# Score matmuls on strips of 32 columns, pads among the last scatters, and the bank of a third tile

## The chip, the cores and the metric

One core of a Trainium2 chip runs one program. The metric is the device time of one execution in microseconds (us), lower is better. TensorE (PE) multiplies, with its weight loads shown apart as PEld; VectorE is DVE, ScalarE is ACT, GpSimd is POOL, and SyncE (SP) issues most of the DMAs. POOL issues the indirect DMAs (scatters) and the pads, on a DMA queue of its own (q0); SP's loads run on q1.

## The reference

The input is `x` of 8 x 2880 tokens with 192 values each. Two steps follow each other:

- a convolution: each of 8 heads weights the last 7 tokens with a softmax over 7 given numbers: `out[s] = sum_k w[s,h,k] * x[s-6+k]`;
- a mixture of experts on the 23040 tokens that come out. `g_logits = x @ w_group` picks one of 4 groups by argmax, `e_logits = x @ w_expert[g]` one of 4 experts in it, so 16 experts in all. The token's result is `relu(x @ w1[g,e]) @ w2[g,e]` (192 to 1024 to 192), times the two softmax weights of the choices.

The choice needs 4 + 16 = 20 scores per token, each a product over 192 values.

## The kernel before, in words

The tokens are taken in 15 groups of 1536 (12 rows of 128 partitions). For each group a front computes the convolution (mostly on DVE), then `logits` (line 387): the rows are turned by TensorE so that the 192 values lie on partitions, values 0 to 127 as one turned tile per row and the remaining 64 of two rows together as a third. `score` multiplies the turned tiles (`xTs`) with the score weights `wr`. `wr[:, 0, :]` are the weights of values 0 to 127, `wr[:, 1, :]` and `wr[:, 2, :]` hold those of the remaining 64 in their upper or lower half and zeros in the other, 32 columns each. In the product the 32 score columns of four rows lie on the four strips of 32 partitions of one bank. `ranks` (line 446) turns scores into a place for each token: a DRAM buffer `rows` holds the tokens sorted by expert, and twelve scatters of POOL (`scatter_row`, line 518, issue line 523) put a group's tokens there. A scatter reads its places from a small copy `ix` (line 522), of which there are three in turn.

`table` (line 537) makes from the counts the list of blocks whose rows are complete at the end of a round (14 rounds; ROUNDS lists at which group each ends and how many blocks of which width it runs). In the last round the remaining rows run, so each expert's run of rows is padded with 256 rows of zeros first: 16 DMAs of POOL (the loop at lines 592 to 598, issue line 595), each with a place read by POOL from a tile `pfi` (line 593).

The blocks run meanwhile, in `blocks` (line 1072). A block loads its rows (`xb`, line 825) and the expert's weights by SP, turns the rows (`prep_x`, line 919; the tile `tpx` or `tp`, transposes at lines 935 and 936), and has two products per unit: `gemm1` (line 961) and `gemm2` (1007, or 1009 and 1010). From round 12 on a block is not `whole`: w2 is loaded into `raw` or `xin` (line 855), cut into a high part by ACT (line 884) and a low part by DVE (line 892). Likewise the turned rows: ACT writes the high part `xh` (line 941), DVE subtracts it and writes the low part `xl` (line 892); both read the bank in which the turned columns lie. A block of three tiles turns two of them at the second unit of the block before it, and the third tile later. Blocks of three tiles are one in round 10 and, in the last round, three full ones and seven with a short third tile; so the last round has nine transitions from a block of three tiles to another.

The order of instructions on PE, ACT, DVE and SP is written out by a planner in the kernel (`clk` holds its clock of each engine, `run` adds a cost, `arrive` says when a round's rows may be loaded); each of these engines runs its list in order. POOL's order is set by the framework from what is ready. Dependencies between the pads and loads of earlier rounds are declared away (`written_once`), so that only the last round's row loads wait for the pads.

Two pieces of code that the change touches:

```python
tp = ps_t.tile([P, 2, 1, P], F32, name="tp") if beside else ps_x.tile([P, 2, 2, P], F32, name="tpx")[:, :, 0:m]
...
if nxt.nt > 2 and u == (last // 2 + 1 if cur.wide else 1):
    prep_x(nxt, 2, not cur.wide)
```

`ps_t` and `ps_x` have one bank each.

Of the kernel before, what the change touches and what calls it, by code (L numbers as in the profile page):

```python
# [12 lines left out]
I32 = mybir.dt.int32  # L13
# [29 lines left out]
def conv_moe_kernel(ctx: ExitStack, tc: tile.TileContext, x, wgen, w_group, w_expert, w1, w2, out):  # L43
# [221 lines left out]
    def run(eng, cost, *deps):  # L265
        clk[eng] = max([clk[eng]] + [d + HOP for d in deps]) + cost
        return clk[eng]
# [10 lines left out]
    def round_of(g):  # L278
        return next(r for r in range(NR) if g < ENDS[r])
# [107 lines left out]
    def logits(g, o):  # L387
        n = WIDTHS[g]
        xrow = o.xrow
        early = g < FIRST  # L390
        pause = lambda t: UNIT if state["begun"] and t > clk["pe"] + 0.9 else NEXT
        yield Chunk(o, 1)
        new_lt = lambda: ps_y.tile([P, SG // 4, P], F32, name="py0") if g == FIRST - 1 else ps_l.tile([P, SG // 4, P], F32, name="pl")
        lt = new_lt() if early else None

        xTs = rt.tile([P, SG // 4, 2, 3, P], F32, name="xT")

        def score(q0, q1):
            for w in range(2):
                nc.tensor.matmul(  # L400
                    lt[2 * w * LW:2 * (w + 1) * LW, q0:q1, :], lhsT=wr[:, 1:3, :].rearrange("p a l -> p (a l)"), rhs=xTs[:, q0:q1, w, 2, :],
                    start=True, stop=False, tile_position=(0, 2 * w * LW))
            for j in range(4):
                nc.tensor.matmul(  # L404
                    lt[j * LW:(j + 1) * LW, q0:q1, :], lhsT=wr[:, 0, :], rhs=xTs[:, q0:q1, j // 2, j % 2, :],
                    start=False, stop=True, tile_position=(0, j * LW))

        txTs, scored = [], 0
        for s2 in range(0, n, 2):
            if o.chunks <= s2 // SC:  # L410
                yield Chunk(o, s2 // SC + 1)
            if s2 % SC == 0:
                rem = rt.tile([P, SC, HP], F32, name="rem")
                nc.scalar.copy(out=rem, in_=xrow[s2 // SC][:, :, P:D])
                txTs += [run("act", 0.4, clk["dve"])] * 2
                yield pause(txTs[-1])
            ttp = run("pe", 0.35, txTs[-2])
            tp = ps_t.tile([P, 3, P], F32, name="tp") if s2 % 4 == 0 else ph_tile(0, [P, 3, P]) if early else ps_l.tile([P, SG // 4, P], F32, name="pl")
            row = xrow[s2 // SC][:, s2 % SC:s2 % SC + 2, :]
            for u in range(2):  # L420
                nc.tensor.transpose(out=tp[:, u, :], in_=row[:, u, 0:P], identity=ident)
            nc.tensor.transpose(out=tp[:, 2, :], in_=rem[:, s2 % SC:s2 % SC + 2, :].rearrange("p s d -> p (s d)"), identity=ident)
            if early and s2 % 4 == 0 and s2:
                run("pe", 0.5, txTs[-1])
                score(s2 // 4 - 1, s2 // 4)
                scored = s2 // 4
            nc.scalar.copy(out=xTs[:, s2 // 4, s2 % 4 // 2], in_=tp)
            txTs.append(run("act", 0.48, ttp))
            yield NEXT if s2 < n - 2 else pause(txTs[-1])
        lt = lt or new_lt()  # L430
        run("pe", 0.1 + 0.4 * (n // 4 - scored), txTs[-1])
        score(scored, n // 4)
        lts = xTs[:, 0].rearrange("p w u t -> p (w u) t")[:, 0:3, :]
        nc.scalar.copy(out=lts, in_=lt)
        tlt = run("act", 0.48, clk["pe"])
        yield pause(tlt)
        lp = ps_l.tile([P, SG // 4, P], F32, name="pl")
        for u in range(n // 4):
            nc.tensor.transpose(out=lp[:, u, :], in_=lts[:, u, :], identity=ident)
        run("pe", 0.35, tlt)  # L440
        ls = rt.tile([P, SG, NL], F32, name="ls")[:, 0:n, :]
        nc.scalar.copy(out=ls, in_=lp.rearrange("p q (j l) -> p (q j) l", l=LW)[:, 0:n, 0:NL])
        run("act", 0.4, clk["pe"])
        ranking.append([ranks(g, o, ls, Until(clk["act"] + LATE[0 if early else 1])), None])

    def ranks(g, o, ls, tls):
# [61 lines left out]
        pi = rt.tile([P, SG], I32, name="posi", bufs=2)[:, 0:n]  # L508
        nc.vector.scalar_tensor_tensor(out=pi, in0=ps, scalar=-1.0, in1=ps, op0=ALU.mult, op1=ALU.max)
        yield TINY  # L510
        for s in range(n):
            run("pool", 2.2 if g in SPACED else 1.28, clk["dve"])
            scatter_row(pi[:, s:s + 1], xrow[s // SC][:, s % SC, :], round_of(g), g in SPACED)
        if g + 1 in ENDS:
            yield from table(round_of(g))
        o.routed = True

    def scatter_row(idx, src, r, spaced):
        ix = idx
        if spaced:  # L520
            ix = new_ix()
            nc.gpsimd.tensor_copy(out=ix, in_=idx)  # L522
        written_once(nc.gpsimd.indirect_dma_start(  # L523
            out=rows[:, :], out_offset=bass.IndirectOffsetOnAxis(ap=ix, axis=0),
            in_=src, in_offset=None, bounds_check=NROW - 1, oob_is_err=False), r)
# [11 lines left out]
    def table(r):  # L537
# [3 lines left out]
        def t(name, shape=(P, NE), dt=F32):  # L541
            return tb.tile(list(shape), dt, name=name)

        if last:
            pfi = t("pfi", (P, NE), I32)
            v.tensor_tensor(out=pfi, in0=cnt.rearrange("p e o -> p (e o)"), in1=lower, op=ALU.add)
        units, n2, tk = t("units"), t("n2"), t("tk")
        v.tensor_tensor(out=units, in0=cnt.rearrange("p e o -> p (e o)"), in1=per_unit, op=ALU.mult)
        v.tensor_tensor(out=units, in0=units, in1=origin[last], op=ALU.add)
# [38 lines left out]
            yield 0.6  # L588

        if last:  # L590
            pad2 = padding()
            for e in range(NE):
                rv = nc.gpsimd.value_load(pfi[0:1, e:e + 1], min_val=0, max_val=NROW - BK)
                run("pool", 1.04, clk["dve"])
                ins = nc.gpsimd.dma_start(out=rows[bass.ds(rv, BK), :].rearrange("(p t) c -> p t c", t=2), in_=pad2)
                written_once(ins, r)
                if e % 4 == 3:
                    yield NEXT
            for nb in (1, 2, 3, *CUT):
                arrive[r, nb] = clk["pool"] + 7.0  # L600

# [470 lines left out]
    def blocks(n0, n1, paced):  # L1072
# [99 lines left out]
        for i in range(len(units) + LAG):  # L1172
            if i < len(units):
                n, u = units[i]
                last = units_of(n) - 1
                gemm1(cur, u)
                queue.append((cur, u))
                nxt_at = i + last + 1 - u
                if nxt_at < len(units):
                    if u == 0:  # L1180
                        pump(units[nxt_at][0])
                        nxt = block(nxt_at)
                        prep_d(nxt)
                    if u == 1:
                        prep_x(nxt, 0)
                    if nxt.nt > 2 and u == (last // 2 + 1 if cur.wide else 1):
                        prep_x(nxt, 2, not cur.wide)
                if u == last and i + 1 < len(units):
                    cur = nxt
            asks = []  # L1190
            if i >= LAG:
                b, u = queue.pop(0)
                gemm2(b, u)
                if u == units_of(units[i - LAG][0]) - 1:
                    finish(b)
                    if b.cut:
                        gemm2_half(b)
                    if i - LAG + 1 < len(units):
                        asks.append(units[i - LAG][0] + 3)
            if i < len(units):  # L1200
                n, at = units[i]
                end = at == last
                if end and n + 4 < n1 and plain(n + 3) and not plain(n + 4):
                    ask_w(n + 4)
                    ask_w(n + 3)
                elif end and n + 3 < n1 and plain(n + 3):
                    ask_w(n + 3)
                elif end and n + 4 < n1 and plain(n + 2):
                    ask_w(n + 4)
                did = 0  # L1210
                for job in list(jobs):
                    m, part, h = job
                    if m > n + 2 or (part == 3 and (m > n + 1 or at < LAG)):
                        continue
                    must = end and m == n + 1
                    if not must and (did >= 1 or (m, part) in want or not ready(m)):
                        continue
                    jobs.remove(job)
                    work_split(job)
                    did += 1  # L1220
                state["unit"] += 1
                state["gemm"] += 1
            flush()
            if paced:
                fill(clk["pe"] + AHEAD[0 if cur.plain else 1 if cur.o.whole else 2])
            for a in asks:
                ask_x(a)
            pump()
# [45 lines left out]
```

## Time and profile before

| | |
|---|---|
| time, three runs | 1169.13, 1172.85, 1174.21 us; median 1172.85 |
| the profiled execution | 1175.43 us; its span from first to last instruction 1173.5 us |
| mean granted TensorE clock | 0.992 of full speed |
| PE busy | 1110.5 us, 95% of the span, 7865 matmul instructions |
| PEld busy | 1032.0 us, 88% |
| DVE busy | 950.4 us, 81% |
| ACT busy | 648.3 us, 55% |
| POOL busy | 580.0 us, 49% |
| DMA | 275.06 MB, mean 234 GB/s |

Busy shares are means over the whole span. An fp32 matmul of the source shows as two instructions, and the end of each is modelled, so the time from the start of one to the start of the next says more than a duration. The row of an instruction ends with the idle time of its engine before it and what released it; a releaser can be named wrongly ("issue" is time for which the profile shows none).

### The profile page before, as it was taken

What the parts mean: (1) busy time and instruction counts of PE and PEld (TensorE: products, weight loads), DVE (VectorE), ACT (ScalarE), POOL (GpSimd) and SP (SyncE); (2) the same over time, 40 slices, a digit from 0 to 9 for tenths busy, and PEclk for the clock granted to TensorE, in tenths of its full rate; (3) what the DMA queues carried; (4) which work ended last, traced back from release to release, by engine and by line L of the source; (5) the groups of instructions that cost most, each with busy time, mean ns of one, the idle gap of its engine ahead of it and who ended that gap; (6) DMA issues with size and microseconds to landing.
All of it is one profiled execution on the core that took longest, in us unless ns stands there. A gap on an engine that the chain in (4) does not pass through costs nothing.

```text
span 1173.5 us, 23791 instructions
## 1 busy us (share of the span) xinstructions
PE 1110.5 (95%) x7865; PEld 1032.0 (88%) x7865; DVE 950.4 (81%) x1682; ACT 648.3 (55%) x1307; POOL 580.0 (49%) x613
## 2 busy tenths in 40 slices
PE   5887998999999999999999999999999899999997
PEld 2444888899999999999999999999899899999997
DVE  8899997989888999989898989998673576655661
ACT  1341445555656555555565566556556676666672
POOL 7064184738256563758483837384746312222211
PEclk9998999999999999999999999999999999999999
DMA  5797999787778786888897868866768885665562
GB/s 175 224 308 221 295 311 297 237 286 226 274 223 265 232 293 216 272 244 262 250 297 221 282 213 270 270 206 195 238 191 231 250 241 159 186 183 192 162 211 68
DMA packets 84343, 275.06 MB, mean 234 GB/s; under 512 B 15297, under 2 KB 34161, under 8 KB 82417
## 3 DMA queue, kind: packets, MB, share of 16 engines
q1 hardware_dynamic: 64056, 229.77, 63.3%
q0 software_dynamic: 20032, 43.39, 12.2%
q8 instruction: 64, 1.05, 0.4%
q14 instruction: 71, 0.57, 0.1%
q10 hardware_dynamic: 120, 0.28, 0.1%
HBM read 225.83 MB, written 47.88 MB: 233 GB/s over the span
## 4 chain that ended last, share of the span: by engine, by line
PE 55%; issue 20%; DVE 10%; DMA 6%; POOL 5%; ACT 2%; another core or an unknown queue 1%; POOLq 1%; SPq 0%; DVEq 0%; ACTq 0%
PE py L1007 25%; PE ph L961 22%; POOL out L1045 5%; DVE pr L317 4%; DMA xin<-in_x 2%; DVE xrow L335 1%; DMA raw<-in_moe_w 1%; PE tpx L936 1%; DMA xb<-rows 1%; PE tpx L935 1%; PE ph L358 1%; PE pl L404 1%; PE pl L400 1%; DMA rows<-rem 1%
## 5 line engine op out<-in xcount | busy, mean ns | idle before, releaser
L961 PE MATMUL ph<-xh,wa 128*128 128x256 f32 (+3 forms) x1992 | 453.4, 303 | 0.0
L1045 POOL DMA_INDIRECT out<-y,xb x189 | 213.2, 1128 | 404.1 <-DVE y L1040 168.4
L1007 PE MATMUL py<-wc,hh 128*128 128x192 f32 x2160 | 399.6, 326 | 3.6 <-ACT y L1034 3.6
L961 PE MATMUL ph<-xl,wa 128*128 128x256 f32 (+3 forms) x1328 | 349.7, 284 | 0.6 <-DVE xl L892 0.6
L1007 PEld LDWEIGHTS py<-wc,hh 128*128 128x128 f32 x2160 | 344.8, 189 | 4.8 <-ACT y L1034 4.6
L961 PEld LDWEIGHTS ph<-xh,wa 128*128 128x128 f32 x1992 | 335.6, 189 | 9.9 <-issue 8.4
L970 ACT ACTIVATE hh<-ph 128x512 f32<-128x512 f32 (+2 forms) x296 | 165.6, 560 | 263.3 <-PE ph L961 218.8
L317 DVE TENSOR_TENSOR pr<-xin,wt 128x1152 f32<-128x1152 f32 x186 | 249.0, 1350 | 4.2 <-PE py L358 3.5
L961 PEld LDWEIGHTS ph<-xl,wa 128*128 128x128 f32 x1328 | 251.0, 189 | 1.0 <-DVE xl L892 0.9
L523 POOL DMA_INDIRECT rows<-xrow,ix x156 | 222.5, 1427 | 47.4 <-POOL ix L522 32.3
L335 DVE TENSOR_TENSOR xrow<-xrow,pr 128x1152 f32<-128x1152 f32 x144 | 194.6, 1351 | 0.7
L892 DVE SCALAR_TENSOR_TENSOR pr<-ph,hh 128x256 fp32r<-128x256 f32 (+2 forms) x128 | 65.7, 514 | 87.0 <-ACT hh L975 37.2
L892 DVE TENSOR_TENSOR wa<-raw,wa 128x1024 fp32r<-128x1024 f32 x83 | 101.3, 1220 | 23.7 <-ACT wa L868 19.4
L522 POOL COPY ix<-posi 128x1 int32<-128x1 int32 x156 | 73.3, 482 | 76.8 <-DMA rows<-xrow,ix 44.5
L1009 PE MATMUL py<-wc,hh 128*128 128x384 f32 x320 | 102.0, 363 | 0.0
L975 ACT ACTIVATE hh<-ph 128x256 fp32r<-128x256 f32 (+2 forms) x128 | 58.9, 460 | 56.9 <-PE ph L961 56.0
L868 ACT CAST wa<-raw 128x1024 fp32r<-128x1024 f32 x83 | 87.2, 1050 | 0.0
L877 ACT CAST wa<-raw 128x1024 fp32r<-128x1024 f32 x83 | 86.7, 1044 | 0.0
L1010 PE MATMUL py<-wc,pr 128*128 128x192 f32 x320 | 80.5, 252 | 0.0
L1034 ACT ACTIVATE y<-py,xb 128x192 f32<-128x192 f32 x175 | 66.3, 426 | 20.0 <-PE py L1007 15.4
L892 DVE TENSOR_TENSOR xl<-tpx,xh 128x512 fp32r<-128x512 f32 (+1 forms) x92 | 59.1, 643 | 13.3 <-ACT xh L941 11.9
L1010 PEld LDWEIGHTS py<-wc,pr 128*128 128x128 f32 x320 | 61.5, 192 | 0.0
(209 smaller groups left out, 1326.3 us busy)
## 6 DMA issues: line engine op xcount, KB each, us to landing
wc<-in_moe_w SPq DMA_DIRECT2D x73, 768.0 KB
raw<-in_moe_w SPq DMA_DIRECT2D x83, 512.0 KB
xin<-in_x SPq DMA_DIRECT2D x14, 1728.0 KB
raw<-in_moe_w SPq DMA_DIRECT2D x91, 256.0 KB
raw<-w1lo SPq DMA_DIRECT2D x83, 256.0 KB
xb<-rows SPq DMA_DIRECT2D x75, 194.0 KB
wa<-in_moe_w SPq DMA_DIRECT2D x24, 384.0 KB
raw<-in_moe_w SPq DMA_DIRECT2D x11, 768.0 KB
```

Source lines behind the costliest of these rows:

```text
L317: nc.vector.tensor_tensor(out=dst, in0=o.xin[:, c0 + k:c0 + k + SC, :].rearrange("p s (h g) -> p s h g", g=HG), in1=w4[:, c0:c0 + SC, :, k ...
L335: nc.vector.tensor_tensor(out=acc, in0=acc, in1=prs[k - 2], op=ALU.add)
L523: written_once(nc.gpsimd.indirect_dma_start(out=rows[:, :], out_offset=bass.IndirectOffsetOnAxis(ap=ix, axis=0), in_=src, in_offset=None, ...
L868: nc.scalar.copy(out=o.wa[:, 0, :], in_=o.raw[0])
L877: nc.scalar.copy(out=o.wa[:, 2, :], in_=o.raw[1])
L892: f(*a, **k)
L961: nc.tensor.matmul(ph[:, v, :], lhsT=w[:, f0:f0 + P], rhs=rhs, start=i == 0, stop=i == len(terms) - 1)
L970: nc.scalar.activation(out=hh, in_=ph, func=AF.Relu)
L1007: nc.tensor.matmul(b.acc[t], lhsT=hh[:, v, c], rhs=wc[0][:, f, :], start=f == 0 and not (b.wide and t == 1), stop=f == NFT - 1 and not (b. ...
L1009: nc.tensor.matmul(b.py[t], lhsT=hh[:, v, c], rhs=wc[f // 4][:, f % 4].rearrange("p l d -> p (l d)"), start=f == 0, stop=False)
L1010: nc.tensor.matmul(b.acc[t], lhsT=hl[:, v, c], rhs=wc[f // 4][:, f % 4, 0, :], start=False, stop=f == NFT - 1)
L1045: ins = nc.gpsimd.indirect_dma_start(out=out[:, :], out_offset=bass.IndirectOffsetOnAxis(ap=b.x.bitcast(I32)[part, t, D + 1:D + 2], axis=0 ...
```

## The change

Three places change. In `score`, the products of the remaining 64 values are no longer two matmuls of 64 columns but four of 32, and run after those of values 0 to 127 instead of before. For the last group, the 16 pads are issued between the scatters (one or two after each of the twelve) instead of after the round's table; `pfi` and the pad tile are made ahead of the scatters, and the planner's cost of a scatter of that group is 1.28 instead of 2.2. The third tile of a block is always turned in the bank of `tp`, also where the block before it has three tiles.

```diff
         def score(q0, q1):
-            for w in range(2):
-                nc.tensor.matmul(
-                    lt[2 * w * LW:2 * (w + 1) * LW, q0:q1, :], lhsT=wr[:, 1:3, :].rearrange("p a l -> p (a l)"), rhs=xTs[:, q0:q1, w, 2, :],
-                    start=True, stop=False, tile_position=(0, 2 * w * LW))
-            for j in range(4):
-                nc.tensor.matmul(
-                    lt[j * LW:(j + 1) * LW, q0:q1, :], lhsT=wr[:, 0, :], rhs=xTs[:, q0:q1, j // 2, j % 2, :],
-                    start=False, stop=True, tile_position=(0, j * LW))
+            for u in range(2):
+                for j in range(4):
+                    nc.tensor.matmul(
+                        lt[j * LW:(j + 1) * LW, q0:q1, :], lhsT=wr[:, u * (1 + j % 2), :], rhs=xTs[:, q0:q1, j // 2, (j % 2, 2)[u], :],
+                        start=u == 0, stop=u == 1, tile_position=(0, j * LW))
...
+        final = g + 1 == ENDS[-1]
+        if final:
+            pfi = tb.tile([P, NE], I32, name="pfi")
+            nc.vector.tensor_tensor(out=pfi, in0=cnt.rearrange("p e o -> p (e o)"), in1=lower, op=ALU.add)
+            pad2 = padding()
         for s in range(n):
-            run("pool", 2.2 if g in SPACED else 1.28, clk["dve"])
+            run("pool", 2.2 if g in SPACED and not final else 1.28, clk["dve"])
             scatter_row(pi[:, s:s + 1], xrow[s // SC][:, s % SC, :], round_of(g), g in SPACED)
+            if final:
+                for e in range(s * NE // n, (s + 1) * NE // n):
+                    rv = nc.gpsimd.value_load(pfi[0:1, e:e + 1], min_val=0, max_val=NROW - BK)
+                    run("pool", 1.04)
+                    ins = nc.gpsimd.dma_start(out=rows[bass.ds(rv, BK), :].rearrange("(p t) c -> p t c", t=2), in_=pad2)
+                    written_once(ins, round_of(g))
...
-            for e in range(NE):
-                rv = nc.gpsimd.value_load(pfi[0:1, e:e + 1], min_val=0, max_val=NROW - BK)
-                run("pool", 1.04, clk["dve"])
-                ins = nc.gpsimd.dma_start(out=rows[bass.ds(rv, BK), :].rearrange("(p t) c -> p t c", t=2), in_=pad2)
-                written_once(ins, r)
-                if e % 4 == 3:
-                    yield NEXT
...
-                        prep_x(nxt, 2, not cur.wide)
+                        prep_x(nxt, 2, True)
```

## Rows read from the trace of the kernel before

**Rows 1.** Windows: from:to, length, busy us of PE, PEld, DVE, ACT, POOL, clock, DMA share, GB/s.
```profile
300.00:600.00 300.00, 298.12 (x2203) 288.14 (x2202) 275.91 (x460) 176.14 (x329) 175.81 (x165) 1.00 0.81 252
966.00:1104.00 138.00, 134.67 (x956) 128.03 (x955) 83.23 (x160) 92.03 (x236) 33.30 (x31) 1.00 0.59 173
```
**Rows 2.** Timeline (start us, length us, engine): PE, one group's scores.
```profile
795.30 0.87 PE L400 MATMUL pl<-xT,wr 128*64 128x384 f32 x4
796.10 0.85 PE L404 MATMUL pl<-xT,wr 128*32 128x384 f32 x8
796.88 0.38 PE L961 MATMUL ph<-xh,wa 128*128 128x256 f32 x1
```
**Rows 3.** Timeline, PEld, the last group's scores.
```profile
845.67 0.16 PEld L404 LDWEIGHTS pl<-xT,wr 128*32 128x32 f32 x8 [0.60 <-issue]
```
**Rows 4.** Source lines 400 and 404: count, ns min/median/max, first and last start, forms.
```profile
L400 PEld LDWEIGHTS pl<-xT,wr x64: 132/134/137, 35.2 to 844.9; 128*64 128x64 f32 x64
...
L404 PEld LDWEIGHTS pl<-xT,wr x128: 106/108/110, 35.6 to 845.7; 128*32 128x32 f32 x128
```
**Rows 5.** Timeline, PE, two first tiles turned, then a third.
```profile
1018.03 0.31 PE L961 MATMUL ph<-xl,wa 128*128 128x320 f32 x1
1018.17 0.27 PE L935 MATMUL tpx<-ident,xb 128*128 128x128 f32 x1
...
1023.99 0.30 PE L961 MATMUL ph<-xl,wa 128*128 128x320 f32 x1
1024.80 0.33 PE L935 MATMUL tpx<-ident,xb 128*128 128x128 f32 x1 [0.50 <-issue]
```
**Rows 6.** Timeline, DVE, the same stretch.
```profile
1022.93 1.22 DVE L892 TENSOR_TENSOR wa<-raw,wa 128x1024 fp32r<-128x1024 f32 x1
1024.06 0.68 DVE L892 TENSOR_TENSOR xl<-tpx,xh 128x512 fp32r<-128x512 f32 x1
1024.66 0.41 DVE L892 SCALAR_TENSOR_TENSOR pr<-ph,hh 128x256 fp32r<-128x256 f32 x1
```
**Rows 7.** Timeline, PE, first transpose for four successive blocks of round 12.
```profile
906.91 0.27 PE L935 MATMUL tpx<-ident,xb 128*128 128x128 f32 x1
...
919.75 0.33 PE L935 MATMUL tpx<-ident,xb 128*128 128x128 f32 x1 [2.58 <-DMA xb<-rows]
...
932.75 0.27 PE L935 MATMUL tpx<-ident,xb 128*128 128x128 f32 x1
...
942.40 0.27 PE L935 MATMUL tpx<-ident,xb 128*128 128x128 f32 x1
```
**Rows 8.** Timeline, ACT, first cast of w2 in three successive blocks.
```profile
904.13 0.83 ACT L884 CAST wc<-raw 128x768 fp32r<-128x768 f32 x1 [3.25 <-DMA raw<-in_moe_w]
...
918.62 0.83 ACT L884 CAST wc<-raw 128x768 fp32r<-128x768 f32 x1 [7.49 <-issue]
...
927.54 0.83 ACT L884 CAST wc<-raw 128x768 fp32r<-128x768 f32 x1 [0.93 <-DMA raw<-in_moe_w]
```
**Rows 9.** Timeline, SP's queue, the loads of w2 for those casts.
```profile
897.18 0.34 SPq L855 DMA_DIRECT2D raw<-in_moe_w  x1
...
908.66 0.34 SPq L855 DMA_DIRECT2D raw<-in_moe_w  x1
...
923.13 0.34 SPq L855 DMA_DIRECT2D raw<-in_moe_w  x1
```
**Rows 10.** DMA view: issues of the pads from 862 to 895, then 895 to 911.
```profile
rows<-rem POOLq DMA_DIRECT2D x5, 194.0 KB
...
rows<-rem POOLq DMA_DIRECT2D x11, 194.0 KB
```
**Rows 11.** Groups by line, POOL, 862 to 912: count, busy, mean ns, idle before.
```profile
L523 POOL DMA_INDIRECT rows<-xrow,ix x12 | 12.0, 998 | 3.5 <-issue 2.7 <-POOL ix L522 0.8
L595 POOL DMA_DIRECT2D rows<-rem x16 | 11.4, 722 | 7.3 <-issue 7.2
...
L522 POOL COPY ix<-posi 128x1 int32<-128x1 int32 x12 | 2.5, 228 | 8.8 <-DMA rows<-xrow,ix 5.2 <-DVE posi L509 3.6
```
**Rows 12.** Window around PE's restart, columns as in rows 1.
```profile
920.00:925.00 5.00, 3.56 (x16) 3.49 (x16) 4.10 (x7) 4.31 (x9) 0.00 (x0) 0.66 0.53 151
```

More of the change, by code (lines that the diff above doesn't have):

```diff
@@ L542, in t @@
             return tb.tile(list(shape), dt, name=name)
-        if last:
-            pfi = t("pfi", (P, NE), I32)
-            v.tensor_tensor(out=pfi, in0=cnt.rearrange("p e o -> p (e o)"), in1=lower, op=ALU.add)
         units, n2, tk = t("units"), t("n2"), t("tk")
@@ L590, in table @@
         if last:
-            pad2 = padding()
-            for e in range(NE):
-                rv = nc.gpsimd.value_load(pfi[0:1, e:e + 1], min_val=0, max_val=NROW - BK)
-                run("pool", 1.04, clk["dve"])
-                ins = nc.gpsimd.dma_start(out=rows[bass.ds(rv, BK), :].rearrange("(p t) c -> p t c", t=2), in_=pad2)
-                written_once(ins, r)
-                if e % 4 == 3:
-                    yield NEXT
             for nb in (1, 2, 3, *CUT):
```

## The prediction, made before the changed kernel ran

> **What bounds the kernel now.** I read the windows first. From 300 to 600 us PE is busy for 298.1 of 300 us, and in the last round, 966 to 1104, for 134.7 of 138 [rows 1]. DVE is close behind in the first stretch (275.9) and far behind in the second (83.2). So what the change takes off PE's list counts in full, and a stall of PE in the later stretch counts in full; the question is how many there are. Two kinds show.
>
> The first is at the third tile. The first two tiles are turned without a gap: the last `gemm1` matmul starts at 1018.03 and the first transpose at 1018.17, 0.14 us later. For the third the same step takes from 1023.99 to 1024.80, 0.81 us [rows 5]. DVE's list says why: the subtraction that reads `tpx` for the first two tiles runs from 1024.06 to 1024.74, behind one for `wa` of 1.22 us that starts at 1022.93 [rows 6]. The bank is free only then, and PE goes on 0.06 us later. The releaser named in that row is "issue", but the bank's reader ends at that very moment. Six blocks show it, one every 13.4 us from 1011 to 1078; the three transitions before them lose little.
>
> The second is in round 12. Its blocks follow each other every 9.65 us (932.75 to 942.40), yet from 906.91 to 932.75 two blocks take 25.84 us: 6.5 us are lost [rows 7]. PE's row at 919.75 names the load of `xb`, but ACT is the earlier clue: it stood 7.49 us before its cast of w2 at 918.62 [rows 8]. That w2 was asked for at 908.66, so it took 9.96 us; the one of 923.13 was there by 927.54, after 4.4 us, and the one of 897.18 took 6.95 us [rows 8, 9]. ACT's next rows, the turned columns' copies and the ReLUs, stand behind that cast, and `xb` behind w2 on SP's queue. In the 33 us before 895 five pads were issued, in the 16 us after it eleven [rows 10]: the pads come in a lump just when the loads of round 12 must be quick. After PE's idle time the granted clock reads 0.66 for 5 us, a mix of its two levels, 1.2 and 2.4 GHz [rows 12]; that is part of the 6.5 us.
>
> **The change part by part.**
>
> *Scores.* Before, one late group's scores take from 795.30 to 796.88, 1.58 us: 0.80 for the 64-column half and 0.78 for the 32-column half [rows 2]. After, both halves are of the second kind: 2 x 0.78 = 1.56 us, less what the switch between the two column widths costs. The row does not part that switch off; I take 0.04 us more, so 0.06 us per group. There are 13 such groups, all under a busy PE: 0.8 us. The first two of the 15 score in smaller pieces in the early stretch and are left out. The lower bound is no gain; the upper 0.1 us a group, 1.3 us. A loss would come if weight loads stopped overlapping.
>
> The eight weight loads of a 32-column half, 0.108 us each, all lie within 0.16 us of the moment at which its first matmul starts [rows 3, 4], so loads and matmuls of different column strips overlap here. The Trainium skill says otherwise: in "TensorE: Matmul & The Clock Gate", Part 3, The mechanism, a weight load overlaps matmuls in flight only when its row group differs, and the four strips share all rows. By that rule the half adds loads to the path; the trace disagrees, and I go by the trace.
>
> *Third tile.* The bank of `tp` is not read by the late subtraction. In the last round its readers are the third tile's own, a block earlier. So the wait goes: six times 0.81 - 0.14 = 0.67 us, 4.0 us. What is late next: DVE's next piece is the low part of a unit's hidden values, at 1024.66 to 1025.07 [rows 6]; `gemm2` needs it two units after the unit's `gemm1`, which leaves PE one `gemm2` and one `gemm1`, over 1 us, before it. PE comes 0.67 us earlier and still finds it done. ACT and the loads follow PE, and the DMA share there is 0.59 [rows 1], so nothing else is near. Bounds: 0 (if something else is late at once) to 4.3 us with the small ones; a loss is excluded, as no reader of the other bank is recent.
>
> *Pads.* POOL's work for the last group is 12 scatters of 1.00 us, 16 pads of 0.72 us and the copies, with idle time before each; 5.2 us of it before the copies, for a scatter's landing, because `ix` has three copies in turn [rows 11]. With a pad or two after each scatter, three scatters and four pads lie between a copy and the landing that it waits for, so that wait should go and the end of the pads come from 911 to about 906. Above all they are spread: 16 in some 44 us, 0.36 per us, where the lump had 11 in 16 us, 0.69 per us. Half of the lump lies elsewhere. Counting w2's delay as proportional, 9.96 - 4.4 = 5.6 us shrinks to 2.9, so ACT waits 7.49 - 2.7 = 4.8 us in place of 7.49. The 3.25 us wait at 904.13 [rows 8] has no loss of this kind behind it: PE turns the next block at 906.91 without idle time [rows 7]. So ACT has that much in hand; what remains for PE is about 4.8 - 3.25 = 1.6 us. So 6.5 - 1.6 = 4.9 us are gained, with the clock's dip in it. The upper bound is 6.5 us. The other one is a loss of as much: the pads that move forward now meet earlier loads of weights, and one more of these may come as late. I take 4.9, nearer to the side where the row of 904.13 stands. Queued behind the pads on POOL are the scatters of finished blocks; they have eight buffers `y`, four blocks of two tiles, about 39 us at 9.65 us a block [rows 7], so PE does not see them. The last round's row loads, which need all pads, belong to blocks that are turned from about 942.40 + 9.65 = 952 us on [rows 7], 40 us after the last pad. `pfi` on DVE only moves.
>
> *Sum.* 0.8 + 4.0 + 4.9 = 9.7 us off the profiled execution's 1175.43 gives 1165.7. That execution was 2.6 us above the median of the three runs, 1172.85; 9.7 off the median is 1163.2 us, my forecast. Its own range, with each part at its bounds but without a loss, is 1160.7 (1.3 + 4.3 + 6.5 off) to 1168.
>
> **The rivals.**
>
> *The lump stays.* POOL's order is the framework's, and it already slots pads between scatters; if POOL is as slow as before, the pads still end near 911 and w2 is as late, or the lateness moves to the load of 897.18, which is already at 6.95 us. Only 4.8 us are gained: 1168.0. For it: 7.2 us of idle time before the pads are named "issue" [rows 11], which no order removes. Against it: the spreading itself.
>
> *Pads too early (slower).* The pads moved ahead now fall on the loads of the last whole blocks and of the first two blocks of round 12. If two more loads of w2 come as late as that of 908.66, and that one stays late, two more losses of 6.5 us come in: 1172.85 - 4.8 + 13 = 1181. It decides from the point where a w2 takes more than 4.4 + 3.25 = 7.7 us from issue to cast with no more time in hand than these; the one of 897.18 is 0.7 us from it. Against it: the loads before 895 have longer leads, and 11 pads were needed to delay one.
>
> *Strips that wait for each other.* If the four strips' weight loads lay on the path, a group would pay 16 x 0.108 in place of 8 x 0.108 + 4 x 0.134 us [rows 4], 0.33 us more, 4.3 us in 13 groups: 1163.2 + 0.8 + 4.3 = 1168.3. Rows 3 speak against it. The Trainium skill's rule named above would give this.
>
> *The third tile's wait only changes its name.* DVE does the same work in the same order; if the next product waits for its low part instead, 4.0 us are lost from the sum: 1167.2. Against it: the 1 us in hand.
>
> **How the numbers follow.** The forecast has 0.50, the lump that stays 0.28, pads too early 0.07, strips 0.06, the renamed wait 0.09. Within 0.5% of 1172.85, that is 1167.0 to 1178.7, a measurement of this kernel can't be told from no change (the three runs span 5.1 us). The forecast gives faster in 0.48 and no change in 0.02; the lump 0.10 and 0.18; the strips 0.02 and 0.04; the renamed wait 0.04 and 0.05; the early pads 0.07 slower. Together 0.64 faster, 0.29 the same, 0.07 slower. For 8 in 10 the range goes from 1158, a little below the forecast's lower bound for the runs' own spread, to 1170, which holds the lump, the strips and the renamed wait with some spread.
>
> **What would show it.** Scores: from the first score matmul to the next work 1.45 to 1.56 us. Third tile: transposes into `tp` within 0.2 us of the last `gemm1` matmul in all nine transitions, and a block of the short kind in 12.7 us rather than 13.4. Pads: even spacing from 863 to about 906, no cast of w2 after more than 5 us of waiting, four blocks of round 12 at about 9.7 us each and a clock near 1 there. It is wrong if one w2 of round 12 is still some 10 us under way, if the block period stays 13.4 us, or if new waits of PE for weights appear between 862 and 900.

## The result and the profile after

The changed kernel takes 1162.45 us (median of 6 runs, 1158.31 to 1163.72), the kernel before 1172.17 us beside it (6 runs, 1168.66 to 1174.21): a ratio of 0.9909, 95% interval 0.9886 to 0.9932. The forecast was 1163.2 us, range 1158 to 1170. Two later comparisons gave 0.9952 and 0.9929 (below), so the gain lies between some 6 and 11 us. The profiled execution took 1161.11 us (span 1159.1), against 1175.43 us (span 1173.5) before.

**Scores.** PE's timeline of one late group, columns as in [rows 2]:

```profile
792.11 1.50 PE L401 MATMUL pl<-xT,wr 128*32 128x384 f32 x16
793.53 0.50 PE L958 MATMUL ph<-xh,wa 128*128 128x256 f32 x2
```

From the first score matmul to the next work there are 793.53 - 792.11 = 1.42 us, in place of 1.58. It is 1.42 to 1.43 us in every late group with PE's work right behind it; in the last group, where PE waits 0.60 us for ACT afterwards, it is 2.10 us in place of 2.25. So a group saves 0.15 us, and 13 groups 2.0 us. The loads, by line (count, ns min/median/max):

```profile
L401 PEld LDWEIGHTS pl<-xT,wr x256: 106/109/110, 35.6 to 842.0; 128*32 128x32 f32 x128
```

A group has 16 of them. One after the other they would take 16 x 0.109 = 1.74 us, more than the whole group takes, so weight loads lie beside other loads and beside matmuls in flight. The Trainium skill, in "TensorE: Matmul & The Clock Gate", Part 3, The mechanism, allows the latter only across row groups; here the four strips share all rows, and the measurement decides against the rule. That it is the matmuls of the other strips that a load lies beside is not shown: from 300 to 600 us, where nearly all weights are 128 columns wide, PE and PEld are both busy over 97% of the time as well (window below).

**Third tile.** PE's timeline where a third tile is turned, the place of the second half of [rows 5], then DVE's of the same stretch, that of [rows 6]:

```profile
1025.81 0.32 PE L958 MATMUL ph<-xl,wa 128*128 128x320 f32 x1
1025.96 0.27 PE L932 MATMUL tp<-ident,xb 128*128 128x128 f32 x1
1026.07 0.27 PE L933 MATMUL tp<-ident,xd 128*128 128x128 f32 x1
1026.10 0.42 PE L1006 MATMUL py<-wc,hh 128*128 128x384 f32 x1
```

```profile
1024.74 1.22 DVE L889 TENSOR_TENSOR wa<-raw,wa 128x1024 fp32r<-128x1024 f32 x1
1025.88 0.68 DVE L889 TENSOR_TENSOR xl<-tpx,xh 128x512 fp32r<-128x512 f32 x1
1026.48 0.41 DVE L889 SCALAR_TENSOR_TENSOR pr<-ph,hh 128x256 fp32r<-128x256 f32 x1
```

The step is 0.15 us now, although DVE reads `tpx` just as late: at 1025.88, after PE's last product of the unit. The transposes no longer ask for that bank. Windows of the first stretch of [rows 1], of 128 us of the last round, and of the 25 us around the stop that is told below (for [rows 12]):

```profile
300.00:600.00 300.00, 299.50 (x2241) 291.23 (x2240) 278.31 (x462) 179.09 (x334) 172.01 (x165) 1.00 0.80 256
962.00:1090.00 128.00, 128.00 (x924) 123.47 (x923) 78.26 (x153) 87.96 (x230) 33.27 (x30) 1.00 0.62 178
900.00:925.00 25.00, 23.48 (x179) 22.74 (x178) 16.11 (x24) 16.28 (x29) 8.09 (x8) 1.00 0.84 249
```

In the last round PE is busy all of the time. The dip of the clock to 0.66 is gone in this execution.

**Pads.** The DMA view of the pads issued from 862 to 895 us (5 in [rows 10]); POOL's groups from 858 to 895, as in [rows 11]; ACT's first casts of w2 in three blocks of round 12; PE's first transposes of four blocks ([rows 8] and [rows 7]):

```profile
rows<-rem POOLq DMA_DIRECT2D x15, 194.0 KB, 7.2
```

```profile
L520 POOL DMA_DIRECT2D rows<-rem x16 | 11.5, 730 | 3.9 <-issue 3.9
L530 POOL COPY ix<-posi 128x1 int32<-128x1 int32 x12 | 3.8, 324 | 3.8 <-DVE posi L506 3.6 <-DMA rows<-xrow,ix 0.2
```

```profile
897.33 0.83 ACT L881 CAST wc<-raw 128x768 fp32r<-128x768 f32 x1 [1.89 <-DMA raw<-in_moe_w]
...
910.64 0.83 ACT L881 CAST wc<-raw 128x768 fp32r<-128x768 f32 x1 [3.35 <-DMA raw<-in_moe_w]
...
919.44 0.83 ACT L881 CAST wc<-raw 128x768 fp32r<-128x768 f32 x1 [1.97 <-DMA raw<-in_moe_w]
```

```profile
902.92 0.33 PE L932 MATMUL tpx<-ident,xb 128*128 128x128 f32 x1 [1.29 <-DMA xb<-rows]
...
913.15 0.27 PE L932 MATMUL tpx<-ident,xb 128*128 128x128 f32 x1
...
923.33 0.27 PE L932 MATMUL tpx<-ident,xb 128*128 128x128 f32 x1
...
932.99 0.27 PE L932 MATMUL tpx<-ident,xb 128*128 128x128 f32 x1
```

The copies' wait for a scatter's landing went from 5.2 to 0.2 us, and the pads' idle time from 7.3 to 3.9, so the pads are over by 894, where the forecast had 906. Some 4.5 us of that are the group's earlier start (POOL's first copy at 858.10 in place of 862.60). ACT's 7.49 us have become 3.35, and the two blocks that took 25.84 us take 20.41. But there is a stop at 902.92 that was not there before, for rows that came late, and the loads behind these are issued later too. SP's queue and POOL's timeline tell why, and the waits of SP's queue from 885 to 925 (us in total, times, longest) name it:

```profile
891.73 0.34 SPq L852 DMA_DIRECT2D raw<-in_moe_w  x1
900.43 0.33 SPq L822 DMA_DIRECT2D xb<-rows  x1
```

```profile
892.51 1.45 POOL L520 DMA_DIRECT2D rows<-rem  x2
894.26 1.04 POOL L1042 DMA_INDIRECT out<-y,xb  x1 [0.30 <-ACT y L1031]
895.61 1.02 POOL L1042 DMA_INDIRECT out<-y,xb  x1 [0.30 <-ACT hh L972]
```

```profile
SPq L822 <- DMA out<-y,xb: 7.6, 1, 7.6
```

The rows of a block go into one of 12 row slots, and the scatter of a finished block (`out`) reads its indices from that slot. The load of `xb` that SP reaches at 893 waits for such a scatter; on POOL it stands behind 12 scatters and 16 pads, and the first `out` since the pads began comes at 894.26. In the kernel before this wait is not among SP's.

### The profile page after: what moved, and what is told of

Its sections match the earlier page's. It is cut to its first block, busy times and chain, and to the rows that moved or that the text cites. A ratio compares the mean times of both kernels' runs of the same rounds, so it can differ in the third digit from the quotient of the medians.

```text
span 1159.1 us, 23947 instructions
## 1 busy us (share of the span) xinstructions
PE 1104.1 (95%) x7941; PEld 1034.3 (89%) x7941; DVE 950.8 (82%) x1682; ACT 648.5 (56%) x1307; POOL 583.6 (50%) x613
## 4 chain that ended last, share of the span: by engine, by line
PE 74%; issue 8%; DVE 7%; DMA 4%; POOL 3%; ACT 2%; POOLq 1%; SPq 1%; DVEq 0%; ACTq 0%
PE ph L958 31%; PE py L1004 26%; PE py L1006 3%; DVE pr L317 3%; PE pl L401 2%; PE py L1007 2%; PE tpx L933 1%; PE tpx L932 1%; POOL out L1042 1%; PE ph L358 1%; DMA xb<-rows 1%; POOL rows L531 1%; DVE pr L353 1%; PE pl L1015 1%; PE tp L418 1%
## 5 line engine op out<-in xcount | busy, mean ns | idle before, releaser
L530 POOL COPY ix<-posi 128x1 int32<-128x1 int32 x156 | 76.2, 500 | 61.7 <-DMA rows<-xrow,ix 31.9
L889 DVE TENSOR_TENSOR xl<-tpx,xh 128x512 fp32r<-128x512 f32 (+1 forms) x83 | 56.5, 681 | 14.6 <-ACT xh L938 14.4
```

The costliest lines, as they stand in the source:

```text
L889: f(*a, **k)
```

## The experiments

Ratios are to the kernel before on the same chip. `outs_between` ran beside the three of one part each; `after_again` beside `slots_14`, `pads_first` and `third_later`; `after_third` beside `pads_act`, `pads_sp` and `wide_second`.

**One part at a time** (`scores_alone`, `third_alone`, `pads_alone`): each is the kernel before with that part of the diff and no other.

> Only the scores change (eight matmuls of 32 columns). Theory: what is saved is the step from one column width to the other, so from the first score matmul to the next work 1.40 us in place of 1.58 in each of 13 groups under a busy PE, 2 us off in all, ratio about 0.998. Rival: the weight loads of the strips lie on the path, 4 us more, ratio 1.004. A second question: the first block of two tiles was turned 3.7 us later in the changed kernel (196.4 against 192.7 us). If the scores of the first two groups cause that, it is here too; if it is the spread of the early DMA loads, it is not tied to this part.

> Only the third tile's bank changes. Theory: the six waits of 0.67 us and the small ones go, 4 to 5 us off, ratio 0.996, block period 12.7 us in place of 13.4. Rival: the wait goes to the next product, which waits for DVE: period 13.4 us and ratio 1.000.

> Only the pads change place. Theory: the loss of 6.5 us in round 12 comes from the lump of pads on the DMA queues while w2 is loaded; with the pads spread, at most 2 us of it remain: 4 to 5 us off, ratio about 0.996, and no load of w2 in round 12 takes over 8 us. Rival: the scatters of finished blocks, now behind 28 operations of POOL, hold rows' slots, and SP waits as long as before: ratio 1.000.

| kernel | us, median | ratio | 95% interval |
|---|---|---|---|
| scores_alone | 1173.86 | 0.9991 | 0.9964 to 1.0019 |
| third_alone | 1168.65 | 0.9956 | 0.9928 to 0.9983 |
| pads_alone | 1172.28 | 0.9970 | 0.9942 to 0.9998 |
| before | 1174.21 | | |

The product of the three is 0.9917, within the interval of the whole, so nothing speaks against the parts adding; each interval is as wide as its part or nearly so, and that of `scores_alone` holds no change. The traces say more than these times. The score groups take 1.43 us in `scores_alone` and 1.58 in the two others, and from the block of 942.40 [rows 7] to the end `third_alone` gains what the changed kernel gains, so those two parts stand each for itself. `pads_alone` has the same new wait; its waits of SP's queue, 885 to 925:

```profile
SPq L825 <- DMA out<-y,xb: 7.6, 1, 7.6
```

and PE stops for it (1.48 us at 906.75) and once more for DVE's `xl` (2.77 us at 916.92): in this execution the pads gained nothing.

**Outs between the scatters** (`outs_between`): the changed kernel, with the planner let in ahead of each scatter of the last group, so that the scatters of two finished blocks slip in between.

```diff
-            run("pool", 2.2 if g in SPACED and not final else 1.28, clk["dve"])
+            yield from ([Until(clk["dve"] + 2.0)] if final and s else []); run("pool", 2.2 if g in SPACED and not final else 1.28, clk["dve"])
```

> The changed kernel, with the planner waiting 2.0 us of its clock after each scatter of the last group and the pads behind it, so that POOL has the scatters of two finished blocks between these. Theory: the stop of 1.9 us at 903 us in the changed kernel comes from SP waiting 7.5 us for such a scatter, queued behind all pads, before it may load a block's rows; here SP's wait is under 1 us and the stop goes: about 2 us less than the changed kernel, ratio about 0.989. Rival: the loads alone set it, and the stop stays at 1 to 3 us: ratio as the changed kernel's, 0.991.

1164.26 us, 0.9924 (0.9895 to 0.9953), an interval that holds the 0.991 of the rival and just misses the 0.989 of the theory. SP waits for no `out` any more and the stop at 903 is gone, but the pads end 10 us later, at 904, and meet w2 again. ACT's cast and PE's restart:

```profile
913.97 0.83 ACT L881 CAST wc<-raw 128x768 fp32r<-128x768 f32 x1 [5.06 <-DMA raw<-in_moe_w]
```

```profile
916.87 0.33 PE L933 MATMUL tpx<-ident,xd 128*128 128x128 f32 x1 [1.28 <-ACT xd L914]
```

So the late `out` does make the stop at 903. With the `out` early, and the pads later for it, this execution stops elsewhere.

**The changed kernel twice more** (`after_again`, `after_third`), as the yardstick of the two later comparisons.

> The changed kernel once more, as the yardstick for the three others on the same chip. Both theories: ratio to the kernel before 0.991 (0.988 to 0.994), some 1163 us. In its profile SyncE should stand about 7.5 us at the load of xb near 893 us, for an out of a finished block, and TensorE lose about 2 us at 903; if an execution shows no such stand, the wait is a matter of that one execution and not of the order of POOL's work.

> The changed kernel as the yardstick for the kernels beside it on the same chip. Both theories: 0.991 to 0.996 of the kernel before, the two ratios found so far. In its profile SyncE stands 7 to 9 us at the load of xb near 893 us for an out of a finished block, and TensorE loses 1.5 to 5 us between 900 and 922.

1171.07 us, 0.9952 (0.9927 to 0.9977), and 1162.03 us, 0.9929 (0.9901 to 0.9957). The first ratio lies outside the 0.988 to 0.994 expected. SP's wait for the `out` stands in both, 9.0 and 6.5 us; the 6.5, and PE's loss with it, are under what the second text expected. PE's row at the stop, of `after_again` and then of `after_third`:

```profile
907.63 0.33 PE L932 MATMUL tpx<-ident,xb 128*128 128x128 f32 x1 [2.97 <-DMA xb<-rows]
```

```profile
898.73 0.33 PE L932 MATMUL tpx<-ident,xb 128*128 128x128 f32 x1 [0.35 <-DMA xb<-rows]
```

With the 1.29 us after 7.6 above these are three executions in one order: 6.5, 7.6 and 9.0 us of SP's wait, 0.35, 1.29 and 2.97 us of PE's. In `after_again` the loss does not end there. The w2 that SP asks for at 908.84, some 12 us after the last pad was issued, is 8.7 us under way:

```profile
917.54 0.83 ACT L881 CAST wc<-raw 128x768 fp32r<-128x768 f32 x1 [4.63 <-DMA raw<-in_moe_w]
```

PE stops once more behind it, 0.92 us at 920.44, and the dip of the clock is back (0.74 from 910 to 915). So a w2 of round 12 can be late with no pad left to issue.

**Fourteen row slots** (`slots_14`): two slots more, for which two of the eight `y` buffers had to go.

```diff
-    NXB = 12
+    NXB = 14
...
-    new_y = ring("y", 8, [P, D])
+    new_y = ring("y", 6, [P, D])
```

> The changed kernel with 14 row slots in place of 12, paid for by six y buffers in place of eight. Theory A (the load of xb stands behind the index of a row slot, which an out scatter queued on POOL behind the pads still has to read): with two more slots SyncE does not stand at 893, the stop of TensorE at 903 goes, and the time is about 2 us below the changed kernel's, ratio to it 0.998. Rival B (the outs' lateness is what counts, whatever they hold): with fewer y buffers gemm2's results wait for the outs instead, TensorE stops there, and the time is the same or up to 4 us more. Rival C (the traffic of pads and loads makes the load late anyway): no stand of SyncE, but xb or w2 still lands late and TensorE loses 1 to 2 us near 903 to 915; time as the changed kernel's.

1174.68 us, 0.9979 (0.9954 to 1.0004), where the changed kernel beside it has 0.9952; the intervals overlap, so slower than it is not sure. Rival B's place is right: SP waits for no `out`, but ACT does, with the next product of PE behind it. ACT, then PE:

```profile
902.94 0.73 ACT L1031 ACTIVATE y<-py,xb 128x192 f32<-128x192 f32 x2 [7.50 <-DMA out<-y,xb]
```

```profile
903.42 0.69 PE L1006 MATMUL py<-wc,hh 128*128 128x384 f32 x1 [6.25 <-ACT y L1031]
```

Whatever the scatter of a finished block holds, slot or buffer, is the next thing missed. Whether 14 slots would help with eight `y` stays untried.

**All pads first** (`pads_first`): the loop of 16 pads stands ahead of the 12 scatters instead of among them.

> The changed kernel with all 16 pads ahead of the last group's scatters (and none among them): on POOL two outs and a few scatters come between the later scatters. Theory A (what costs is that pads meet round 12's loads, and that the outs of the blocks stand behind them): the pads are over by about 880, w2 of round 12 takes under 6 us, SyncE does not stand for an out near 893, and the time is 1 to 3 us below the changed kernel's, ratio to it 0.998. Rival B (it is the even spread that helps, and a lump costs wherever it lies): a new stop of TensorE of 2 to 6 us between 862 and 895, with a w2 of the blocks there 8 us or more under way; the time is 2 to 4 us above the changed kernel's, about that of the kernel with two parts and old pads, 1167.

1177.00 us, 0.9998 (0.9966 to 1.0029): by the medians 5.9 us more than the changed kernel beside it, so the pads' gain is lost. Neither theory has the place right. The pads are over by 893 (expected: 880), SP waits for no `out`, and no w2 of round 12 lets ACT wait over 2.8 us. PE stops at 850, ahead of the first pad, for 3.4 us. That stop is not of the pads' order: `scores_alone`, with the old pads, has one of 3.23 us at the same product (851.56). From 933 to 936 PE stops five times for 0.3 to 0.9 us, with "issue" as the releaser; the scatters that had been pushed back run to 926, and outs to 934. The profile doesn't say what is late there, and why this kernel is slower stays open.

**Pads from other queues** (`pads_act`, `pads_sp`): as `outs_between`, with the pads issued from ACT's or SP's queue.

```diff
-                    rv = nc.gpsimd.value_load(pfi[0:1, e:e + 1], min_val=0, max_val=NROW - BK)
-                    run("pool", 1.04)
-                    ins = nc.gpsimd.dma_start(
+                    rv = nc.scalar.value_load(pfi[0:1, e:e + 1], min_val=0, max_val=NROW - BK)
+                    ins = nc.scalar.dma_start(
```

(`nc.sync` in the other.)

> The changed kernel with the 16 pads issued from ScalarE's queue instead of POOL's, a scatter and one or two pads at a time with the planner's other work between them. The bytes are the same, POOL is rid of 16 x 1.2 us. Theory A (what is left of the loss in round 12 comes from POOL's queue: the outs stand behind scatters and pads): POOL is through with the last scatter before 890, SyncE stands for no out, TensorE loses under 1 us between 895 and 925, and the time is 2 to 4 us below the changed kernel's, ratio to it 0.998 to 0.996. Rival B (the pads' traffic makes w2 and the rows late, whoever issues it): ScalarE still waits 5 us or more for a w2 of round 12 and the time is that of the changed kernel or, with ScalarE held up by the issuing, up to 3 us more.

> As the kernel with pads from ScalarE's queue, but from SyncE's, where they stand among the loads of weights and rows. Theory A: as there, 2 to 4 us below the changed kernel's, since POOL is as free. Rival B: a pad ahead of a load on the same queue delays it by the pad's own transfer, 0.8 us at 250 GB/s each; the loads of xb or w2 between 865 and 895 then land late and TensorE loses 2 to 5 us there, and the time is up to 3 us above the changed kernel's.

1165.83 us, 0.9962 (0.9945 to 0.9979), and 1166.93 us, 0.9984 (0.9964 to 1.0005): by the medians 3.8 and 4.9 us more than the changed kernel beside them (the interval of `pads_act` overlaps that kernel's), and more than the up to 3 us of rival B. With POOL free, SP waits for no `out`, and in `pads_act` round 12 runs as theory A has it: ACT's waits for w2 are 0.56 to 1.44 us. The time is lost earlier, where rival B looked for it, but at a higher price than it gave: the issuing itself holds an engine up. ACT's timeline in `pads_act`, four pads and then the next work, and SP's in `pads_sp`, four pads and then a load of rows:

```profile
879.54 4.71 ACTq L519 DMA_DIRECT2D rows<-rem  x4
884.29 0.41 ACT L913 COPY xd<-xb 128x256 f32<-128x256 f32 x1 [5.03 <-DMA rows<-rem]
```

```profile
886.86 4.92 SPq L519 DMA_DIRECT2D rows<-rem  x4
892.64 0.35 SPq L821 DMA_DIRECT2D xb<-rows  x1
```

PE stops 4.30 us for that copy and 3.61 us for those rows. Such a stop also gives the loads of round 12 time to run ahead, so `pads_act` does not show what round 12 would do without it.

**The third tile one unit later** (`third_later`): the kernel before, old bank, with `u == last // 2 + 2` in place of `last // 2 + 1` in wide blocks.

> The kernel before, with old scores, old pads and the old bank for the third tile, which is only turned one unit later in wide blocks. Theory A (the 0.67 us before the third tile is the wait for VectorE's late reader of the bank of the turned columns): one unit later that reader has ended, no gap stands before the transposes, the blocks of the last round come every 12.7 us as with the other bank, and the ratio to the kernel before is 0.9957 (0.993 to 0.998). Rival B (the wait is for something that moves along, PE's own queue or the load of the third tile's rows): the gap of 0.8 us moves one unit on and the time stays that of the kernel before.

1172.07 us, 0.9975 (0.9945 to 1.0006): an interval that holds the 0.9957 expected and no change. The trace tells the two theories apart. PE's timeline:

```profile
1023.91 0.31 PE L961 MATMUL ph<-xl,wa 128*128 128x320 f32 x1
1024.06 0.27 PE L935 MATMUL tpx<-ident,xb 128*128 128x128 f32 x1
```

0.15 us into the same `tpx`, and a block every 12.68 us (1016.78 to 1080.16 in five). So what PE waited for is the reader of the bank, which a later unit finds done.

**The wide half second** (`wide_second`): the kernel before with the four matmuls of 32 columns ahead of the two of 64.

> The kernel before with the two halves of the scores exchanged: the four matmuls of 32 columns first, then the two of 64. Theory A (a group's gain of 0.15 us comes from there being no matmuls of 64 columns, with the change of width in the middle and at the end): first score matmul to next work stays 1.58 us, within 0.03. Rival B (what costs is that narrow matmuls follow wide ones into the same strips): 1.43 to 1.50 us, as with eight narrow ones. The time itself is not told apart by one execution.

One execution, 1166.93 us. PE's timeline of a late group:

```profile
792.62 0.85 PE L400 MATMUL pl<-xT,wr 128*32 128x384 f32 x8
793.41 0.87 PE L404 MATMUL pl<-xT,wr 128*64 128x384 f32 x4
794.20 0.50 PE L961 MATMUL ph<-xh,wa 128*128 128x256 f32 x2
```

Again 1.58 us: the 0.15 us hang on the 64-column matmuls being there, not on their order. Whether the wide matmuls themselves or the two changes of width cost it, this does not part. The numbers favour the changes: eight instructions of 32 columns between two changes take 0.78 us first or second, and eight more without a change between add 1.43 - 0.78 = 0.65. So one change less is worth some 0.13 us (an estimate), and the 64-column half itself, 0.80 against 0.78, the other 0.02.

## Why the prediction was right, and where its terms were not

The total was right, 9.7 us forecast and 1172.17 - 1162.45 = 9.7 measured at first. The terms were not, and their errors cancel, so that the total came out is luck: by the ratios of the three comparisons the gain is 10.7, 5.7 and 8.3 us, some 8.2 on average. The range told with the sum, 1160.7 to 1168 "with each part at its bounds", is wrong at its upper end: no gain from any part, which the bounds allow, is 1172.85, and 1168 is the rival of the lump. The table parts the spans at the first transposes of two blocks: the last before the last group's pads (838.30 before) and the one of 942.40 [rows 7].

| us | to 838.30 | to 942.40 | to the end |
|---|---|---|---|
| before | 838.30 | 104.10 | 231.1 |
| after | 834.95 | 98.04 | 226.1 |
| after_again | 836.89 | 103.01 | 225.8 |
| after_third | 831.70 | 97.24 | 226.0 |

- **Scores**: 2.0 us against 0.8. A group was to save 0.06 us, 0.02 by the narrower matmuls and 0.04, guessed, by the width switch; it saves 0.15, above the bound of 0.1. By the estimate at `wide_second` the switch is worth 0.13, three times the guess. The rest of the first column's differences is not the change's: the block that comes at 192.70 us before comes at 196.43 in the changed kernel, but at 199.02 in `third_alone`, which changes nothing until then.
- **Third tile**: 5.0 to 5.3 us (5.1) against 4.0, in all three executions, and above the upper bound of 4.3. This stretch repeats: 230.7 to 231.2 us in the four kernels with the old bank at the old unit (`before`, `scores_alone`, `pads_alone`, `wide_second`), 225.5 to 226.2 in the ten others. The mechanism is as told, and `third_later` confirms it. The block's period falls from 13.39 to 12.67 us, 0.72 rather than 0.67; the first of the six transitions gives 0.99, and the earlier ones of the last round, which I had left out of the 4.0, 0.5 together.
- **Pads**: 4.9 us forecast. Timed, `pads_alone` says 0.003 x 1174 = 3.5 us (0.2 to 6.8); the three comparisons of the whole leave 3.6, -1.4 and 1.2 once 2.0 and 5.1 are taken off. About 2 us, then, and never sure in one execution: the middle column has 97.2 to 103.0 with the new pads (105.2 in `pads_alone`), and with the old ones 104.1, 105.0 (`scores_alone`), 100.9 (`third_alone`), 103.9 (`third_later`) and 98.3 (`wide_second`). The w2 half of the mechanism holds: ACT's longest wait for a w2 of round 12 is 5.58 to 7.61 us in the five executions with the old pads, 3.34 to 4.63 in the four with the new ones (4.8 was said). The step that failed is "they have eight buffers `y`, four blocks of two tiles, about 39 us at 9.65 us a block, so PE does not see them". I counted what the outs write from and forgot what else they hold: the row slots of `xb`, whose indices they read. SP stood 6.5 to 9.0 us for one, and PE lost 0.35 to 2.97 us at the stop. The loads that SP issues behind that stand come late as well, and `after_again` shows what that can cost: its middle stretch is only 1.1 us shorter than before.
- **Rivals**: strips that wait for each other and a renamed wait of the third tile are out. [rows 3] shows eight loads beside each other and not, as the prediction reads it, which matmuls they lie beside; that they are off the path is shown by the 1.43 us. The lump that stays is out too, since the pads are over 17 us earlier (911 to 894); that one comparison came to its 5 us goes with SP's stand, as `after_again` shows. "Pads too early" did not come with the change, though it came in another form where pads were issued from SP's or ACT's queue.

No kernel tried beats the changed one; `outs_between`, 0.9924, lies among its three ratios. POOL's order, the outs, and w2 draw on the same stretch. While the pads run, the DMA engines are busy nearly all of the time, by the share ahead of the last column of the changed kernel's windows; around the stop they are not, as the two windows of `after_again` behind them show:

```profile
862.00:874.00 12.00, 12.00 (x91) 12.00 (x90) 11.21 (x67) 7.04 (x14) 8.33 (x13) 1.00 0.93 285
874.00:886.00 12.00, 12.00 (x89) 12.00 (x89) 3.97 (x7) 7.25 (x13) 9.47 (x15) 1.00 1.04 280
886.00:898.00 12.00, 12.00 (x93) 12.00 (x91) 5.59 (x7) 7.08 (x12) 9.92 (x12) 1.00 0.93 281
```

```profile
898.00:910.00 12.00, 8.92 (x65) 8.52 (x65) 6.05 (x8) 5.51 (x10) 9.02 (x8) 0.97 0.61 199
910.00:922.00 12.00, 11.08 (x78) 10.85 (x78) 6.53 (x11) 6.66 (x12) 1.95 (x2) 0.89 0.84 237
```

That the traffic as such sets the floor is not shown: no run took bytes away, and while SP stands the engines have room.

## What to carry to other kernels

When work is moved ahead on an in-order queue, list for each instruction that it passes everything that this one still holds, the buffers that it reads its indices from too, and count each pool's slack; the smallest decides, not the one that comes to mind. A wait for a bank can be removed by another bank or by a later turn, and the trace shows that both do the same. A sum that comes out right says little about its terms: the stretches of the trace that belong to one part each showed two too small and one too large, where times of whole executions could not.

## What the runs showed of the hardware

- Score matmuls on four column strips of 32 run beside each other: 16 of 384 columns in 1.43 us, 0.09 us each, where a 128x128 one of 384 columns takes 0.20 us to the next start (899.98 to 900.18 in the changed kernel). Their 16 weight loads of 0.109 us, 1.74 us in sum, lie inside the same 1.43 us; a mix with 64-column ones costs 0.15 us more for the same result.
- A pad of 194 KB held POOL for 0.73 us; issued from ACT or SP it held that engine's queue some 0.56 us when alone and 1.2 us each when four followed each other.
- The first block of two tiles comes at 192.2 to 199.0 us in kernels that are alike up to there but for the scores of two groups, and the changed kernel's stretch around round 12 takes 97.2 to 103.0 us from one execution to the next; a part worth under 5 us is told from one profile only by a stretch that repeats closely, as the scores (1.42 to 1.43 us) and the third tile's block (12.67 us) do.
